# Conversion of the channel weights in 256-column pieces, spread over two token mixings, with two of its operations on ScalarE

## The chip, the cores and the metric

One core of a Trainium2 chip runs the whole program. The metric is device time in microseconds of one execution, the median of several. The engines named here: TensorE (PE) multiplies matrices into PSUM, VectorE (DVE), ScalarE (ACT) and GpSimd (POOL) work element by element, SyncE (SP) issues DMAs; ScalarE's queue issues some too. Every engine takes its own instructions in the order in which they are queued; semaphores hold an instruction until what it needs is there.

## What is computed

The reference has three stages, one behind the other, on 4 batches of 576 tokens and 512 columns: windowed attention, a mixture of four attention experts, and a mixing layer. The change lies in the last one:

```python
def _moe2_ref(x, w_theta, w_tok_r, w_tok_i, w_ch) -> np.ndarray:
    theta = x @ w_theta
    cos_t, sin_t = (np.cos(theta), np.sin(theta))
    zr = x * cos_t
    zi = x * sin_t
    yr = np.einsum('ts,bsd->btd', w_tok_r, zr)
    yi = np.einsum('ts,bsd->btd', w_tok_i, zi)
    y = yr + yi
    u = x + y
    return (u + np.maximum(u @ w_ch, 0.0)).astype(np.float32)
```

`w_ch`, the channel weights, is 512x512. Its inputs here are 64-bit floating-point numbers, and so are those of `w_theta` and of the token weights.

## The kernel before

Every product is made of three matmuls (`mm3`, L92 to L95): both operands are split into a high part and a low part (`split`, L85 to L90, or the end of `load64`), and high x high, high x low and low x high add up in PSUM. So each operand of a product costs a cast and a subtraction on the helper engines.

The mixing layer works per batch b and per half dh of the columns. `x_split(b)` makes high and low parts of x (tiles cx: L89 on VectorE, L90 on GpSimd). `theta(b, dh)` (L469 to L519) does blocks i of 128 tokens: the angle in PSUM (th, 12 matmuls), a transposed x (xk, a pair of transposes, L486), the fraction of the angle (ang, L490 and L492 on VectorE), sine and cosine on ScalarE (L493 to L495), their products with x (zf, L508 or L517 on VectorE), and the split of these into z (L87 on ScalarE, L90 on GpSimd). `mix(b, dh)` (L521 to L542) multiplies the z blocks by the token weights wkh, wkl into four PSUM banks (y, 108 matmuls), adds them to x on VectorE (L541) and splits the sum (tiles cu). `channel(b)` (L544 to L557) multiplies the sum by the channel weights wch, wcl, of which two of the four row blocks lie in the tiles wd.

`load64` (L100 to L132) turns 64-bit weights into a high and a low 32-bit part. A DMA brings a piece into the tile st (names w64c for the channel weights, w64k for token weights, w64t for theta weights); `lo` and `hi` are its 32-bit halves. Then:

- L115 on GpSimd or L117 on ScalarE: t = hi scaled (`KN["DM"][kind]` decides)
- L118 on ScalarE: u = lo scaled
- L119 and L120 on VectorE: t shifted, and the sign put back
- L122 on GpSimd: t += u, as integers
- L125 on VectorE or L127 on ScalarE: the high part, a cast of t (`KN["DH"][kind]`)
- L128: the low part, t minus the high part (`KN["DL"][kind]`, VectorE for the channel weights)

`KN["DP"][kind]` says into how many column parts a piece is cut for these. Kind 0 is theta, 1 token, 2 channel weights; the token weights go in rows of 576 columns. `load_ch` (L577 to L587) loads the channel weights in eight pieces k of 256 columns. Even and odd pieces have one buffer each: st and t, u of an even piece lie together in one tile (tag bmsx, named w64c), those of an odd piece in two tiles (tags VD0 and VD1, named w64c and wtuc). So a piece's load waits for the end of the piece two before it. The loads are issued from ScalarE's queue (L103).

What is put side by side is decided by `merge` (L45): it draws from generators in turn by their declared costs, which gives the program order and the order in which buffers are handed out. A scheduler of the framework then orders each engine's queue by its own estimate of when an instruction could start. Before the change, all eight pieces are merged with the first mixing:

```python
        todo = [(KN["TC"][4], mix(b, 0)), (KN["TC"][b % 2], theta(b, 1))]
        if b == 0:
            todo.append((KN["CW"][3], load_ch()))
        merge(*todo)
```

In names such as zf0121 or ang012 the digits are b, dh and the block i; in w64c6 and wtuc7 the digit is the piece.

Of the kernel before, what the change touches and what calls it, by code (L numbers as in the profile page):

```python
# [23 lines left out]
DM = H * D  # L24
E = 4
NP = H // 2
KN = {'AT': [12.51, 2.36, 85.51, 5.66, 48.01, 55.86, 30.7, 4.07], 'QK': [16.78, 11.97, 9.28, 7.37, 6.82, 0.65, 9.6, 19.46, 20.6], 'VG': [6.74, 4.28, 3.79, 19.87], 'WO': [16.49, 4.2, 5.44, 88.79], 'PA': [20.87, 6.19, 12.47, 3.34, 11.04, 2.93, 5.67], 'TW': [1.13, 0.05, 2.9, 0.49, 1.86], 'CW': [14.78, 12.49, 0.79, 3.08, 1.4, 0.05, 1.33], 'SC': [5, 4, 3, 3, 0, 5, 1, 1], 'BD': [2, 1, 2, 1], 'PV': [0, 1, 1, 1], 'VB': [4, 0, 0, 2], 'WB': [0, 0, 0, 1], 'SB': 2, 'TB': 3, 'WOI': 0, 'AS': [0, 2, 1, 2], 'WE': [[0, 0], [0, 3], [0, 1]], 'XE': [0, 1, 1, 0], 'QB': [0, 1, 0, 0, 0, 0, 0, 0], 'DM': [1, 0, 1], 'DH': [1, 0, 1], 'DL': [0, 0, 1], 'BC': [1, 0, 1, 1], 'LT': 2, 'DP': [1, 1, 2], 'KC': 0, 'WM': 448, 'TC': [6.98, 7.5, 7.5, 7.5, 20.8, 9.0]}
NZ = 7
CT = ("tb", "bs")
WARM = 2  # L30
# [10 lines left out]
def f32(ap):  # L41
    return ap.bitcast(F32)


def merge(*parts):  # L45

    live = [[0.0, float(total), gen] for total, gen in parts]
    while live:
        p = min(live, key=lambda x: x[0] / x[1])
        cost = next(p[2], None)  # L50
        if cost is None:
            live.remove(p)
        else:
            p[0] += cost
# [3 lines left out]
def kernel(ctx, tc, qT, kT, vw, consts, w_in, w_o, w_th, w_tk, w_ch, outT):  # L58
# [41 lines left out]
    def load64(kind, st, tu, dst_h, dst_l, src, scale=1.0):  # L100
# [7 lines left out]
        lo, hi = v[:, :, 0], v[:, :, 1]  # L108
        n = KN["DP"][kind]
        step = st.shape[1] // n  # L110
        full = lo, hi, tu[:, 0], tu[:, 1], dst_h, dst_l
        for k in range(n):
            lo, hi, t, u, dst_h, dst_l = (x[:, step * k : step * k + step] for x in full)
            if KN["DM"][kind]:
                nc.gpsimd.tensor_scalar(out=f32(t), in0=f32(hi), scalar1=2.0**-112, scalar2=1.0, op0=ALU.mult, op1=ALU.mult)  # L115
# [141 lines left out]
    QS, KA, VG, GW, O = {}, {}, {}, {}, {}  # L257
# [263 lines left out]
    def mix(b, dh):  # L521
        x2 = x2T[b]
        if dh == 0:
            UH[b] = hl_set(utags, f"cu{b}")
        uh, ul = UH[b]
        y = [bank([P, 288], tag, f"y{b}{dh}{k}") for k, tag in enumerate(("g", "g", "as", "ta"))]
        for c in range(9):
            zt = Z[b, dh, c // 2]
            q = c % 2 if c < 8 else 0
            for k in range(4):  # L530
                n, mm = divmod(k, 2)
                sl = slice(288 * n, 288 * n + 288)
                ms = slice(mm * P, mm * P + P)
                mm3(y[k], zt[:, q, 0, ms], zt[:, q, 1, ms], wkh[c][:, sl], wkl[c][:, sl],
                    c == 0, c == 8)
            yield 1.45
        for k in range(4):
            n, mm = divmod(k, 2)
            m = 2 * dh + mm
            sl = slice(288 * n, 288 * n + 288)  # L540
            nc.vector.tensor_add(out=x2[:, m, sl], in0=y[k], in1=x2[:, m, sl])  # L541
            split(uh[m][:, sl], ul[m][:, sl], x2[:, m, sl], nc.scalar, nc.gpsimd)  # L542
# [34 lines left out]
    def load_ch():  # L577
        for k in range(2 * NC):
            c, sl = k // 2, slice(HW * (k % 2), HW * (k % 2) + HW)
            if k % 2:  # L580
                st = bp.tile([P, HW], U64, tag="VD0", name=f"w64c{k}")
                tu = bp.tile([P, 2, HW], U32, tag="VD1", name=f"wtuc{k}")
            else:
                su = rp.tile([P, 2, HW], U64, tag="bmsx", name=f"w64c{k}")
                st, tu = su[:, 0], su[:, 1].bitcast(U32).rearrange("p (two n) -> p two n", two=2)
            load64(2, st, tu, wch[c][:, sl], wcl[c][:, sl], w_ch[c * P : (c + 1) * P, sl])
            yield 0.5  # L587
# [17 lines left out]
    for b in range(B):  # L605
        todo = [(KN["AT"][2 * b], attn(b, 0)), (KN["QK"][2 * b], qk(b, 1))]
# [25 lines left out]
        todo = [(KN["AT"][2 * b + 1], attn(b, 1))]  # L632
# [17 lines left out]
    wd = [bp.tile([P, 2, DM], F32R, tag="vg", bufs=2, name=f"wd{c}") for c in range(2)]  # L650
    wch = [wc[0], wc[2], wd[0][:, 0], wd[1][:, 0]]
    wcl = [wc[1], wc[3], wd[0][:, 1], wd[1][:, 1]]
    for b in range(B):
        todo = [(KN["TC"][4], mix(b, 0)), (KN["TC"][b % 2], theta(b, 1))]
        if b == 0:
            todo.append((KN["CW"][3], load_ch()))
        merge(*todo)
        if b < B - 1:
            x_split(b + 1)
            merge((KN["TC"][4], mix(b, 1)), (KN["TC"][2 + b % 2], theta(b + 1, 0)))  # L660
        else:
            merge((13, mix(b, 1)))
        merge((12, channel(b)))
# [55 lines left out]
```

## Time and profile before

| | before |
|---|---|
| median of 3 runs | 552.16 us (551.96 to 552.63) |
| profiled execution | 552.61 us, its span 550.7 us |
| PE busy | 519.8 us, 94% |
| DVE busy | 367.4 us, 67% |
| ACT busy | 319.1 us, 58% |
| POOL busy | 302.8 us, 55% |
| TensorE clock granted, mean | 0.981 of full speed |

The profiled execution is one run; its span goes from the first to the last instruction that the profile shows, and the rest of its time lies around that. The shares are means over stages with different limits, so the rows below are taken from the stretch in which the channel weights are converted, some 317 to 359 us after the span's start. An engine is shown as busy while an instruction runs or stands in a port; on TensorE shown lengths overlap, since the next matmul starts before the last has drained.

### The profile page before, as it was taken

To read this page: it belongs to the slowest core of one execution; us is meant where nothing else is said; L and a number is where in the kernel's file an instruction comes from. 1 tells how busy PE (TensorE), PEld (TensorE's weight loads), DVE (VectorE), ACT (ScalarE), POOL (GpSimd) and SP (SyncE) were. 2 spreads that over 40 slices of the span, in tenths; PEclk is the share of its full clock that TensorE was granted. 3 is DMA by queue.
4 is the path that set the end of the run, shared out by engine and by line. 5 is a ranking of instruction groups with operands and counts; after the bars stand their busy time and mean duration, and the time that the engine had idled before them with its cause. 6 is when DMAs were issued, how large, how long until landed. Compare 5 with 4: busy or idle time off the path is not lost.

```text
span 550.7 us, 12516 instructions
## 1 busy us (share of the span) xinstructions
PE 519.8 (94%) x4372; PEld 483.6 (88%) x4372; DVE 367.4 (67%) x1394; ACT 319.1 (58%) x1023; POOL 302.8 (55%) x479
## 2 busy tenths in 40 slices
PE   7799999999999999998898998699999999999997
PEld 5679878898987899988787997599999999999997
DVE  5796889858888688659999699953453535443312
ACT  6967687855778667777657955343343414442410
POOL 5786697635757653238565586943364514651420
PEclk9979999999999999999799899989999999999999
DMA  8754233323124331104004112001100110011002
GB/s 273 221 161 134 74 101 89 91 75 106 38 75 130 98 121 32 30 3 129 1 2 149 63 39 72 7 1 35 53 2 0 34 55 1 1 33 55 1 1 87
DMA packets 20799, 36.81 MB, mean 67 GB/s; under 512 B 2304, under 2 KB 13056, under 8 KB 20736
## 3 DMA queue, kind: packets, MB, share of 16 engines
q1 hardware_dynamic: 19008, 31.55, 18.5%
q10 hardware_dynamic: 1728, 4.46, 2.5%
q8 instruction: 35, 0.57, 0.5%
q14 instruction: 28, 0.23, 0.1%
HBM read 31.28 MB, written 4.72 MB: 65 GB/s over the span
## 4 chain that ended last, share of the span: by engine, by line
PE 69%; DVE 18%; ACT 4%; DMA 3%; POOL 3%; issue 3%; SPq 1%; POOLq 0%; ACTq 0%; DVEq 0%
PE y L94 6%; PE y L93 6%; PE y L95 6%; PE as L214 4%; PE ao L249 3%; PE c L94 3%; PE c L95 3%; PE c L93 3%; PE o L424 3%; PE th L93 3%; PE th L95 3%; PE th L94 3%; PE apt L239 2%; PE bpt L409 2%; PE qk L93 2%
## 5 line engine op out<-in xcount | busy, mean ns | idle before, releaser
L90 POOL TENSOR_TENSOR z<-zf,z 128x256 fp32r<-128x256 f32 x72 | 52.9, 751 | 89.8 <-ACT z L87 89.7
L93 PE MATMUL y<-wkh,z 128*128 128x288 f32 x288 | 86.9, 303 | 0.3 <-DVE x2T L541 0.3
L94 PE MATMUL y<-wkl,z 128*128 128x288 f32 x288 | 85.8, 298 | 0.0
L95 PE MATMUL y<-wkh,z 128*128 128x288 f32 x288 | 85.0, 299 | 0.0
L227 ACT ACTIVATE ams<-ams,anm 128x128 f32<-128x128 f32 x144 | 56.9, 398 | 7.6 <-DVE anm L219 6.3
L493 ACT ACTIVATE ang<-ang 128x256 f32<-128x256 f32 x36 | 14.6, 416 | 74.4 <-DVE ang L492 74.2
L93 PEld LDWEIGHTS y<-wkh,z 128*128 128x128 f32 x288 | 54.8, 190 | 0.8 <-DVE x2T L541 0.8
L94 PEld LDWEIGHTS y<-wkl,z 128*128 128x128 f32 x288 | 54.8, 190 | 0.0
L95 PEld LDWEIGHTS y<-wkh,z 128*128 128x128 f32 x288 | 54.4, 190 | 0.0
L384 ACT ACTIVATE bms<-bms,bnm 64x64 f32<-64x64 f32 (+4 forms) x80 | 44.7, 561 | 14.1 <-DVE bnm L376 7.0
L82 POOL TENSOR_SCALAR QD<-qt 64x192 f32<-64x192 f32 x72 | 39.2, 545 | 23.8 <-PE as L214 20.5
L234 POOL TENSOR_TENSOR ams<-ams,arc 128x384 f32<-128x384 f32 x48 | 40.2, 838 | 22.1 <-DVE arc L233 8.1
L87 ACT CAST z<-zf 128x256 fp32r<-128x256 f32 x72 | 27.2, 404 | 40.5 <-PE y L95 15.6
L214 PE MATMUL as<-kt,QD 128*128 128x128 f32 x288 | 43.6, 288 | 4.4 <-ACT QD L209 3.6
L214 PEld LDWEIGHTS as<-kt,QD 128*128 128x128 f32 x288 | 36.3, 192 | 8.8 <-ACT QD L209 3.9
L376 DVE CUSTOM_DVE_ANT_0 bms<-bs,mb 128x288 f32<-128x288 f32 (+4 forms) x96 | 38.8, 426 | 5.8 <-PE bs L374 3.3
L508 DVE TENSOR_TENSOR zf<-xk,ang 128x256 f32<-128x256 f32 x64 | 24.8, 417 | 25.1 <-ACT ang L495 21.1
L93 PE MATMUL th<-wth,cx 128*128 128x256 f32 x128 | 36.5, 286 | 3.8 <-DVE ang L492 3.7
L219 DVE CUSTOM_DVE_ANT_0 ams<-as,cst 128x128 f32<-128x128 f32 x144 | 34.5, 283 | 6.4 <-PE apt L239 5.0
L554 DVE SCALAR_TENSOR_TENSOR x2T<-c,x2T 128x288 f32<-128x288 f32 x32 | 14.4, 456 | 34.6 <-PE c L95 34.5
L94 PE MATMUL th<-wtl,cx 128*128 128x256 f32 x128 | 36.0, 282 | 0.0
L490 DVE TENSOR_SCALAR ang<-th 128x256 f32<-128x256 f32 x36 | 15.1, 420 | 31.2 <-PE th L95 30.9
(196 smaller groups left out, 1778.0 us busy)
## 6 DMA issues: line engine op xcount, KB each, us to landing
vt<-in_dram SPq DMA_DIRECT2D x48, 192.0 KB, 2.4
kt<-in_dram SPq DMA_DIRECT2D x16, 320.0 KB, 3.6
qt<-in_dram SPq DMA_DIRECT2D x16, 288.0 KB, 3.2
out_dram<-x2T SPq DMA_DIRECT2D x32, 144.0 KB, 1.8
w64k<-in_dram SPq DMA_DIRECT2D x5, 576.0 KB, 3.8
w64k<-in_dram ACTq DMA_DIRECT2D x4, 576.0 KB, 3.7
w64t<-in_dram SPq DMA_DIRECT2D x4, 512.0 KB, 4.8
w64c<-in_dram ACTq DMA_DIRECT2D x8, 256.0 KB, 2.8
```

Source lines behind the costliest of these rows:

```text
L82: nc.gpsimd.tensor_scalar(out=out, in0=in_, scalar1=by, scalar2=1.0, op0=ALU.mult, op1=ALU.mult)
L87: nc.scalar.copy(out=dst_h, in_=src)
L90: eng_l.tensor_sub(out=dst_l, in0=src, in1=f32(dst_h))
L93: nc.tensor.matmul(out, wh, xh, start=first, stop=False)
L94: nc.tensor.matmul(out, wh, xl, start=False, stop=False)
L95: nc.tensor.matmul(out, wl, xh, start=False, stop=last)
L214: nc.tensor.matmul(s[:, i, :], QD[g][:, i], kt[:, 64 * blk : 64 * blk + 128], start=True, stop=True)
L219: nc.vector.tensor_tensor_reduce(out=ms[:, i, :], in0=s[:, i, :], in1=ma0 if (g == 0 and i == 0) else ma1, scale=-0.125, scalar=3.0e38, op ...
L227: nc.scalar.activation(out=ms[:, i, :], in_=ms[:, i, :], func=AF.Exp, bias=nm[:, i : i + 1], scale=-1.0, accum_out=sm[:, i : i + 1],)
L234: nc.gpsimd.tensor_mul(out=ms, in0=ms, in1=rc.unsqueeze(2).to_broadcast([P, 3, P]))
L376: nc.vector.tensor_tensor_reduce(out=ms[:m, a:z], in0=s[:m, : z - a], in1=mb[:m, mo + a : mo + z], scale=-0.125, scalar=3.0e38, op0=ALU.ad ...
L384: ex = nc.scalar.activation(out=ms[:m, :w], in_=ms[:m, :w], func=AF.Exp, bias=nm[:m, 0:1], scale=-1.0, accum_out=sm[:m, i : i + 1])
```

## The change

Three entries of the table KN change, each for kind 2, the channel weights: `'DM'` from `[1, 0, 1]` to `[1, 0, 0]` (the scaling of hi goes from GpSimd, L115, to ScalarE, L117), `'DH'` from `[1, 0, 1]` to `[1, 0, 0]` (the cast goes from VectorE, L125, to ScalarE, L127), and `'DP'` from `[1, 1, 2]` to `[1, 1, 1]` (256 columns in one instruction, not twice 128). And `load_ch` is drawn from in two merges, three pieces in the first and the rest in the second:

```diff
@@ -650,14 +650,18 @@
     wd = [bp.tile([P, 2, DM], F32R, tag="vg", bufs=2, name=f"wd{c}") for c in range(2)]
     wch = [wc[0], wc[2], wd[0][:, 0], wd[1][:, 0]]
     wcl = [wc[1], wc[3], wd[0][:, 1], wd[1][:, 1]]
+    ch = load_ch()
     for b in range(B):
         todo = [(KN["TC"][4], mix(b, 0)), (KN["TC"][b % 2], theta(b, 1))]
         if b == 0:
-            todo.append((KN["CW"][3], load_ch()))
+            todo.append((KN["CW"][3], islice(ch, 3)))
         merge(*todo)
         if b < B - 1:
             x_split(b + 1)
-            merge((KN["TC"][4], mix(b, 1)), (KN["TC"][2 + b % 2], theta(b + 1, 0)))
+            todo = [(KN["TC"][4], mix(b, 1)), (KN["TC"][2 + b % 2], theta(b + 1, 0))]
+            if b == 0:
+                todo.append((KN["CW"][3], ch))
+            merge(*todo)
         else:
             merge((13, mix(b, 1)))
         merge((12, channel(b)))
```

On VectorE, the end of the first mixing and the split of the next batch's x, where the last pieces are converted. Before:

```order
L541 TENSOR_TENSOR x2T0_68<-y003_5297,x2T0_68 128x288
L120 SCALAR_TENSOR_TENSOR w64c6_5673<-w64c6_5673 128x128
L89 CAST cx10_5706<-x2T1_69 128x512
L125 CAST wd1_5285<-wtuc7_5690 128x128
L89 CAST cx12_5708<-x2T1_69 128x512
L128 TENSOR_TENSOR wd1_5285<-wtuc7_5690,wd1_5285 128x128
L89 CAST cx14_5710<-x2T1_69 128x512
L490 TENSOR_SCALAR ang012_5508<-th013_5576 128x256
L125 CAST wd1_5285<-w64c6_5673 128x128
L128 TENSOR_TENSOR wd1_5285<-wtuc7_5690,wd1_5285 128x128
L490 TENSOR_SCALAR ang014_5655<-th014_5639 128x256
L492 TENSOR_TENSOR ang012_5508<-th013_5576,ang012_5508 128x256
```

After, from the same addition on:

```order
L541 TENSOR_TENSOR x2T0_68<-y003_5297,x2T0_68 128x288
L89 CAST cx10_5602<-x2T1_69 128x512
L89 CAST cx12_5604<-x2T1_69 128x512
L89 CAST cx14_5606<-x2T1_69 128x512
L508 TENSOR_TENSOR zf0120_5494<-xk012_5484,ang012_5487 128x256
L508 TENSOR_TENSOR zf0121_5498<-xk012_5484,ang012_5487 128x256
L490 TENSOR_SCALAR ang012_5487<-th013_5538 128x256
L128 TENSOR_TENSOR wd1_5285<-w64c6_5827,wd1_5285 128x256
L490 TENSOR_SCALAR ang014_5584<-th014_5568 128x256
L492 TENSOR_TENSOR ang012_5487<-th013_5538,ang012_5487 128x256
L492 TENSOR_TENSOR ang014_5584<-th014_5568,ang014_5584 128x256
```

Of the conversion one subtraction is left behind the addition of y003, where five instructions of it stood in these rows and more behind them; the casts L125 are gone, and the two products zf012 now stand behind the casts of cx, where they stood just ahead of this addition.

On ScalarE, where the last two pieces are loaded and scaled. Before:

```order
L87 CAST z010_5332<-zf0100_5333 128x256
L87 CAST z010_5332<-zf0101_5337 128x256
L118 ACTIVATE wtuc7_5690<-w64c7_5689 128x128 x2
L103 DMA w64c6_5673<-in_8_dram 128x256
L87 CAST z011_5431<-zf0110_5432 128x256
L87 CAST z011_5431<-zf0111_5436 128x256
L493 ACTIVATE ang012_5508<-ang012_5508 128x256
L118 ACTIVATE w64c6_5673<-w64c6_5673 128x128 x2
L494 ACTIVATE ang012_5508<-ang012_5508 128x256
L495 ACTIVATE ang012_5508<-ang012_5508,halfpi_64 128x256
```

After, the same place:

```order
L127 CAST wd0_5284<-w64c4_5699 128x256
L117 ACTIVATE wtuc7_5903<-w64c7_5902 128x256
L118 ACTIVATE wtuc7_5903<-w64c7_5902 128x256
L495 ACTIVATE ang010_5326<-ang010_5326,halfpi_64 128x256
L87 CAST z010_5332<-zf0101_5337 128x256
L103 DMA w64c6_5827<-in_8_dram 128x256
L87 CAST z011_5417<-zf0110_5418 128x256
L87 CAST z011_5417<-zf0111_5422 128x256
L117 ACTIVATE w64c6_5827<-w64c6_5827 128x256
L118 ACTIVATE w64c6_5827<-w64c6_5827 128x256
L127 CAST wd1_5285<-wtuc7_5903 128x256
```

The load of piece 6 (L103) now stands behind both scalings of piece 7, and behind it come L117, L118 and the cast L127, in one queue with the casts of z and the sines.

On GpSimd, from the first split of the sum (cu) in batch 0 to the third z block. Before:

```order
L115 TENSOR_SCALAR w64c6_5673<-w64c6_5673 128x128 x2
L122 TENSOR_TENSOR wtuc7_5690<-wtuc7_5690 128x128 x2
L90 TENSOR_TENSOR cu01_5287<-x2T0_68,cu00_5286 128x288
L122 TENSOR_TENSOR w64c6_5673<-w64c6_5673 128x128
L90 TENSOR_TENSOR cu03_5289<-x2T0_68,cu02_5288 128x288
L90 TENSOR_TENSOR cu01_5287<-x2T0_68,cu00_5286 128x288
L90 TENSOR_TENSOR cx17_5713<-x2T1_69,cx16_5712 128x512
L90 TENSOR_TENSOR z012_5514<-zf0120_5515,z012_5514 128x256
L90 TENSOR_TENSOR z012_5514<-zf0121_5519,z012_5514 128x256
L122 TENSOR_TENSOR w64c6_5673<-w64c6_5673 128x128
L90 TENSOR_TENSOR cu03_5289<-x2T0_68,cu02_5288 128x288
L90 TENSOR_TENSOR cx11_5707<-x2T1_69,cx10_5706 128x512
```

After, from the add of piece 6 on:

```order
L122 TENSOR_TENSOR w64c6_5827<-w64c6_5827 128x256
L90 TENSOR_TENSOR cu01_5287<-x2T0_68,cu00_5286 128x288
L90 TENSOR_TENSOR cu03_5289<-x2T0_68,cu02_5288 128x288
L90 TENSOR_TENSOR cx17_5609<-x2T1_69,cx16_5608 128x512
L90 TENSOR_TENSOR cx11_5603<-x2T1_69,cx10_5602 128x512
L90 TENSOR_TENSOR cu01_5287<-x2T0_68,cu00_5286 128x288
L90 TENSOR_TENSOR cx13_5605<-x2T1_69,cx12_5604 128x512
L90 TENSOR_TENSOR cu03_5289<-x2T0_68,cu02_5288 128x288
L90 TENSOR_TENSOR cx15_5607<-x2T1_69,cx14_5606 128x512
L90 TENSOR_TENSOR z012_5493<-zf0120_5494,z012_5493 128x256
L90 TENSOR_TENSOR z012_5493<-zf0121_5498,z012_5493 128x256
```

The add of piece 6 is one instruction and stands ahead of all splits, where two halves of it were spread among them; the third z block now stands behind the splits of cx.

## Rows read from the trace of the kernel before

**Rows 1.** Page, part 2: busy tenths of TensorE and VectorE, granted clock, in 40 slices

```profile
PE   7799999999999999998898998699999999999997
...
DVE  5796889858888688659999699953453535443312
...
PEclk9979999999999999999799899989999999999999
```

**Rows 2.** Two stretches: from:to, length, busy PE, PEld, DVE, ACT, POOL (instructions), clock, DMA

```profile
321.40:358.00 36.60, 29.30 (x216) 27.58 (x215) 36.26 (x92) 16.75 (x50) 30.05 (x51) 0.99 0.14 44
375.00:550.70 175.70, 172.56 (x1339) 172.32 (x1337) 67.49 (x160) 55.80 (x141) 65.74 (x82) 1.00 0.08 28
```

**Rows 3.** TensorE's timeline: start, length, line, output <- inputs, shape [idle before]

```profile
321.53 0.38 PE L93 MATMUL y<-wkh,z 128*128 128x288 f32 x1
...
332.76 0.30 PE L93 MATMUL y<-wkh,z 128*128 128x288 f32 x1
...
335.68 0.29 PE L94 MATMUL y<-wkl,z 128*128 128x288 f32 x1
...
352.22 0.29 PE L95 MATMUL y<-wkh,z 128*128 128x288 f32 x1
356.23 0.38 PE L93 MATMUL th<-wth,cx 128*128 128x256 f32 x1 [3.72 <-DVE ang L492]
...
358.43 0.44 PE L93 MATMUL y<-wkh,z 128*128 128x288 f32 x1
358.67 0.44 PE L94 MATMUL y<-wkl,z 128*128 128x288 f32 x1
...
361.06 0.38 PE L486 MATMUL xk<-cst,x2T 128*128 128x128 f32 x2
```

**Rows 4.** One stretch, busy by line, in turn L119, L120, L125, L128, L115, L122, L118

```profile
317.10:358.60 41.50, 7.13 (x16) 0.98 0.13 39
...
317.10:358.60 41.50, 5.89 (x16) 0.98 0.13 39
...
317.10:358.60 41.50, 7.42 (x16) 0.98 0.13 39
...
317.10:358.60 41.50, 8.76 (x16) 1.41 (x1) 0.98 0.13 39
...
317.10:358.60 41.50, 4.77 (x16) 0.98 0.13 39
...
317.10:358.60 41.50, 7.57 (x16) 0.98 0.13 39
...
317.10:358.60 41.50, 4.05 (x16) 0.98 0.13 39
```

**Rows 5.** Groups of the page's part 5, then by tile (min/median/max ns)

```profile
L90 POOL TENSOR_TENSOR z<-zf,z 128x256 fp32r<-128x256 f32 x72 | 52.9, 751 | 89.8 <-ACT z L87 89.7
...
L87 ACT CAST z<-zf 128x256 fp32r<-128x256 f32 x72 | 27.2, 404 | 40.5 <-PE y L95 15.6
...
L508 DVE TENSOR_TENSOR zf<-xk,ang 128x256 f32<-128x256 f32 x64 | 24.8, 417 | 25.1 <-ACT ang L495 21.1
...
L119 DVE TENSOR_SCALAR w64c<-w64c x8: 210/314/1420, 317.3 to 346.2; 128x128 uint32<-128x128 uint32 x8
...
L120 DVE SCALAR_TENSOR_TENSOR w64c<-w64c x8: 276/280/565, 318.9 to 348.8; 128x128 uint32<-128x128 uint32 x8
...
L119 DVE TENSOR_SCALAR wtuk<-wtuk x9: 445/450/1090, 246.8 to 311.4; 128x576 uint32<-128x576 uint32 x9
```

**Rows 6.** ScalarE's timeline, two loads of pieces; page, part 6, the loads

```profile
322.98 0.33 ACTq L103 DMA_DIRECT2D w64c<-in_dram  x1
...
342.45 0.33 ACTq L103 DMA_DIRECT2D w64c<-in_dram  x1
...
w64c<-in_dram ACTq DMA_DIRECT2D x8, 256.0 KB, 2.8
```

**Rows 7.** VectorE's timeline, one cast of the split of x

```profile
349.00 1.02 DVE L89 CAST cx<-x2T 128x512 fp32r<-128x512 f32 x1
```

More of the change, by code (lines that the diff above doesn't have):

```diff
@@ L26 @@
 NP = H // 2
-KN = {'AT': [12.51, 2.36, 85.51, 5.66, 48.01, 55.86, 30.7, 4.07], 'QK': [16.78, 11.97, 9.28, 7.37, 6.82, 0.65, 9.6, 19.46, 20.6], 'VG': [6.74, 4.28, 3.79, 19.87], 'WO': [16.49, 4.2, 5.44, 88.79], 'PA': [20.87, 6.19, 12.47, 3.34, 11.04, 2.93, 5.67], 'TW': [1.13, 0.05, 2.9, 0.49, 1.86], 'CW': [14.78, 12.49, 0.79, 3.08, 1.4, 0.05, 1.33], 'SC': [5, 4, 3, 3, 0, 5, 1, 1], 'BD': [2, 1, 2, 1], 'PV': [0, 1, 1, 1], 'VB': [4, 0, 0, 2], 'WB': [0, 0, 0, 1], 'SB': 2, 'TB': 3, 'WOI': 0, 'AS': [0, 2, 1, 2], 'WE': [[0, 0], [0, 3], [0, 1]], 'XE': [0, 1, 1, 0], 'QB': [0, 1, 0, 0, 0, 0, 0, 0], 'DM': [1, 0, 1], 'DH': [1, 0, 1], 'DL': [0, 0, 1], 'BC': [1, 0, 1, 1], 'LT': 2, 'DP': [1, 1, 2], 'KC': 0, 'WM': 448, 'TC': [6.98, 7.5, 7.5, 7.5, 20.8, 9.0]}
+KN = {'AT': [12.51, 2.36, 85.51, 5.66, 48.01, 55.86, 30.7, 4.07], 'QK': [16.78, 11.97, 9.28, 7.37, 6.82, 0.65, 9.6, 19.46, 20.6], 'VG': [6.74, 4.28, 3.79, 19.87], 'WO': [16.49, 4.2, 5.44, 88.79], 'PA': [20.87, 6.19, 12.47, 3.34, 11.04, 2.93, 5.67], 'TW': [1.13, 0.05, 2.9, 0.49, 1.86], 'CW': [14.78, 12.49, 0.79, 3.08, 1.4, 0.05, 1.33], 'SC': [5, 4, 3, 3, 0, 5, 1, 1], 'BD': [2, 1, 2, 1], 'PV': [0, 1, 1, 1], 'VB': [4, 0, 0, 2], 'WB': [0, 0, 0, 1], 'SB': 2, 'TB': 3, 'WOI': 0, 'AS': [0, 2, 1, 2], 'WE': [[0, 0], [0, 3], [0, 1]], 'XE': [0, 1, 1, 0], 'QB': [0, 1, 0, 0, 0, 0, 0, 0], 'DM': [1, 0, 0], 'DH': [1, 0, 0], 'DL': [0, 0, 1], 'BC': [1, 0, 1, 1], 'LT': 2, 'DP': [1, 1, 1], 'KC': 0, 'WM': 448, 'TC': [6.98, 7.5, 7.5, 7.5, 20.8, 9.0]}
 NZ = 7
```

## The prediction

> **What bounds the kernel now.** I read the page's forty slices first, then the busy time of two stretches, then TensorE's timeline with its waits. In slices 24 to 26 (about 317 to 358 us) VectorE shows 9 and TensorE falls from 9 to 6; after that TensorE stays at 9 into the last slice and VectorE at 5 or below [rows 1]. The stretches say the same: from 321.4 to 358.0 VectorE is busy 36.26 of 36.6 us and TensorE 29.30; from 375 on TensorE is busy 172.56 of 175.7 [rows 2]. So VectorE bounds one stretch of some 37 us, and TensorE everything behind it: a microsecond won back in the stretch is a microsecond off the end, one won later is none.
>
> How much is to be won? TensorE's longest wait there, 3.72 us, is for the angle of L492 [rows 3]. Busy time hides part of the loss, since a matmul's shown length overlaps the next, so I count from start to start. An undisturbed y matmul of 288 columns comes every 0.133 us (332.76 to 335.68 is 22 steps), a theta matmul of 256 columns by width every 0.118. From the first y matmul at 321.53 to the transpose pair at 361.06, 39.5 us, TensorE did 159 y matmuls (21.1), 52 theta matmuls (6.1) and seven transpose pairs (1 to 1.5): 28.5 us of work, 11 us lost [rows 3]. The loss has two kinds: waits for VectorE (4.0 us from 352.22 to 356.23 alone), and, behind that long wait, a stretch at the lower clock, 1.2 instead of 2.4 GHz, in which a y matmul takes 0.24 instead of 0.133 us (358.43 to 358.67), some 1.5 us over fourteen of them [rows 1, 3].
>
> **The change part by part.** *VectorE.* Before, eight pieces in two halves give 16 instructions each of L119, L120, L125 and L128: 7.13 + 5.89 + 7.42 + 8.76 = 29.2 us of the stretch's 41.5 [rows 4]. After, the cast L125 is ScalarE's, and 8 each of L119, L120 and L128 remain, twice as wide: 64 instructions become 24. Undisturbed, L119 costs 0.21 us at 128 columns and 0.445 at 576, so 0.28 at 256; L120 costs 0.276 at 128 and, like the 256-column zf of L508, 0.41 to 0.42 at 256; L128 reads two SBUF sources like L120, so the same [rows 5]. That is 8 x (0.28 + 0.42 + 0.42) = 9.0 us as the lower bound. The sixteen sets of before would undisturbed be 16 x (0.21 + 0.276 + 0.21 + 0.276) = 15.6, so 13.6 us of the 29.2 were stretching, 0.21 per instruction. If the stretching goes with the count: 9.0 + 24 x 0.21 = 14 us. If it goes with the length: 9.0 x 29.2/15.6 = 16.8, the upper bound. I take 14, because the same L119 at 576 columns has a median hardly over its minimum (450 against 445) while at 128 it has 314 against 210 and up to 1420: it is not length that stretches [rows 5]. VectorE is thus relieved of about 15 us (12 to 20) in the stretch that it bounds.
>
> A 128-column L119, 210 ns at best, took up to 1420 [rows 5]. The Trainium skill (SBUF — State Buffer, Who interferes with whom) calls the port pair that VectorE shares with GpSimd an exclusive lock, held for a whole instruction while the other blocks. That speaks against wider pieces: all three instructions left can meet the lock, and the GpSimd add that blocks them grows from 0.47 to 0.75 us. By that rule the 0.21 would grow to 0.34 and the 14 us to 17, at the upper bound, and the gain by some 2 us smaller, inside the range; the 1420 ns agree that whole instructions block.
>
> *GpSimd* loses the 16 multiplies of L115 (4.77 us) and does 8 adds of 256 columns for 16 of 128: by the 0.751 us of its 256-column z instruction 6.0 for 7.57 [rows 4, 5]. It gets 6.3 us back.
>
> *ScalarE* does 8 multiplies L117, 8 L118 and 8 casts L127 of 256 columns at the 0.404 us of its z cast: 9.7 us for the 4.05 of before [rows 4, 5]. The 5.7 us more lie beside 16.75 busy of 36.6 us [rows 2], so they cost nothing as a sum. As an order they do: L117 now waits at the head of ScalarE's queue for a piece's load, with z casts and sines queued behind it.
>
> *The spread.* Three pieces belong to the first mixing and five to the second now. The order shows that this moves little: the scheduler sets pieces 3 to 7 where they stood, the last one still in front of the angles of the fourth and fifth theta blocks on VectorE. I cost it at nothing either way (at most one piece, 3 x 0.6 = 1.8 us of VectorE). No DMA is added; the eight loads stay on ScalarE's queue, 2.8 us from issue to landing each [rows 6].
>
> **What is late next.** Two pieces are under way at a time, each in its own buffer, so a load waits until the piece two before is done. Even pieces were loaded at 322.98 and, two trips later, at 342.45: 9.7 us a trip [rows 6]. A trip of after is at least 2.8 (landing) + 0.40 (L117) + 0.28 + 0.42 (L119, L120) + 0.75 (add) + 0.40 (cast) + 0.42 (L128) = 5.5 us; on VectorE a pair of zf (0.83) and of angle steps (0.83) queue between, and z work on ScalarE and GpSimd, so I take 7.8. From 322.98, itself 1.5 earlier since the first piece loses a pair of VectorE steps, the last load is issued at 321.5 + 2 x 7.8 = 337.1 to 338.5 with some queueing behind L117 on ScalarE; I take 338.5, or 8.5 us a trip.
>
> Now VectorE in the new order: landing 341.3, L117 to 341.7, then L119, four additions L541 (0.47 by width), L120 and a stretched L128 to 344.9. Three casts L89, 1.02 us in the row, say 0.9, make 347.6, two zf 348.4; L490, L128, L490, L492 make 350.4 [rows 5, 7]. TensorE gets to the second half's first y matmul at 321.5 + 108 x 0.133 + 48 x 0.118 + six transpose pairs = 342.6. It waits there for the banks that L541 frees (0.9 us in all), stands before the transpose of the fifth block at 346.3 until 348.5 (2.1), and before the first theta block of batch 1 from 349.8 to 350.4 (0.6). So 3.6 us of waits remain, with small ones 4, none long enough to be like the 4.0 us behind which the clock fell. Lost before 11, after 4: **7 us won**. Behind the stretch TensorE is full as before, and the helpers have as much room as before, so all of it arrives at the end. The weights are then ready at about 350, with most of the second mixing's 108 matmuls (14 us) still to come before the channel stage asks for them.
>
> **The rivals.** *The last load comes no earlier* (342.3, two trips of 10.4, where before has 9.7): because L117 makes ScalarE wait for each load, and the next load is issued from that same queue. Everything that hangs on it is 3.8 us later, gain 3.2: 549. For it: loads are issued in order with z casts. Against it: each trip loses two VectorE steps and half its instructions.
>
> *TensorE becomes the bound sooner.* If casts and conversions are hardly stretched, the waits shrink. GpSimd then limits: behind the last add (343.1) stand four cu (0.84 each by width), four cx (1.5) and the first z of the third block (0.75), to 353, where TensorE by the reckoning above arrives at 355. So at most 2 us more: gain 9, 543.2.
>
> *ScalarE's queue turns the change into a loss.* If a trip grows past 12 us (the 7 us spread over two trips on the 8.5 of the forecast), because z casts stand behind L117 and L117 behind a load, the waits in front of the theta block cost more than now; at 13 us a trip it ends 2 us slower, 554.2. For it: 24 conversion instructions on one in-order queue where there were 16 short ones. Against it: ScalarE sits half idle there and its waits are for VectorE.
>
> *The change doesn't do what it says*: the pieces stay in place by the order, and if VectorE's relief were swallowed by stretching, the time would stay at 552.2. Against it: 40 instructions are gone from a full engine.
>
> **How the numbers follow.** The profiled execution took 552.61 us (span 550.7), the median of the runs is 552.16. 552.61 - 7.0 = 545.6, and set against the median 545.2, which I give. Chances: forecast 0.60 (gain 5.5 to 8.5), last load no earlier 0.15, TensorE sooner the bound 0.15, no effect 0.05, slower 0.05. The range from 542.5 to 549.5 takes in the first three with their bounds, VectorE's 12 to 20 us among them, and leaves out little over 0.1. What can be told from no change is about 0.2%, 1.1 us: faster 0.90, the same 0.05, slower 0.05.
>
> **What the changed profile would show.** Right: L119, L120 and L128 of the pieces together 14 us on VectorE (9 to 17) in 24 instructions; the last load at 338.5; TensorE's wait for L492 under 1 us; the clock full around 350; the first channel matmul some 7 us earlier than before. Wrong: the last load at 342 or later (the first rival); z casts that wait on ScalarE behind L117 while TensorE waits for z (the third); or later waits on TensorE behind 358, which would give back what the stretch won.

## The result and the profile after

The changed kernel takes 547.26 us (median; 546.12 to 548.62), the kernel before 552.14 beside it: ratio 0.9905 (0.9877 to 0.9932). The gain is 4.9 us by the medians, 5.9 by the profiled executions (546.72 against 552.61). The forecast was 7.0 us: the sign and the range hold, and the gain is smaller.

The page of the changed kernel, part 2, answers to [rows 1]: slices 24 to 26, where VectorE stood at 9 and TensorE fell to 6, are at 8, 6, 8 and 9, 9, 7, and behind them TensorE is at 9 as before.

```profile
PE   7879999999999999999799899799999999999997
...
DVE  5886898857888688658989868863354435443412
...
PEclk8989999999999999999799899999999999999999
```

The two stretches of [rows 2], with the same columns (the second starts at the same time and ends with the span):

```profile
321.40:358.00 36.60, 33.08 (x257) 32.25 (x256) 29.36 (x61) 21.50 (x61) 29.84 (x36) 1.00 0.14 45
375.00:544.70 169.70, 166.50 (x1293) 166.26 (x1291) 65.47 (x156) 54.48 (x138) 64.21 (x80) 1.00 0.08 28
```

VectorE has come down from 36.26 to 29.36 us, ScalarE has gone up from 16.75 to 21.50, and TensorE does 257 recorded matmuls in the stretch where it did 216. The conversion's part of VectorE, by line L119, L120 and L128 (busy time and count), answers to [rows 4]; L125 has no row any more:

```profile
317.10:375.00 57.90, 3.21 (x8) 1.00 0.09 31
...
317.10:375.00 57.90, 4.93 (x8) 1.00 0.09 31
...
317.10:375.00 57.90, 5.60 (x8) 1.27 (x1) 1.00 0.09 31
```

That is 13.7 us for 29.2. ScalarE's three lines of it (L117, L118, L127) take 3.52 + 3.40 + 3.17 = 10.1 us, GpSimd's add L122 5.92. The last load, from ScalarE's queue, and TensorE's waits from 310 to 400 us (sum, times, longest):

```profile
338.62 0.33 ACTq L103 DMA_DIRECT2D w64c<-in_dram  x1
...
PE xk L486 <- DVE zf L508: 2.7, 1, 2.7
PE th L93 <- DVE ang L492: 0.5, 1, 0.5
PE y L93 <- DVE x2T L541: 0.3, 1, 0.3
```

Where before the longest wait was the 3.72 us for L492 [rows 3], now it is one of 2.7 us for a product zf, in front of the transposes of the fifth theta block. VectorE's timeline says why, with GpSimd's beside it:

```profile
344.07 0.81 DVE L541 TENSOR_TENSOR x2T<-y,x2T 128x288 f32<-128x288 f32 x2
344.80 3.90 DVE L89 CAST cx<-x2T 128x512 fp32r<-128x512 f32 x3
348.62 0.74 DVE L508 TENSOR_TENSOR zf<-xk,ang 128x256 f32<-128x256 f32 x2
349.28 0.41 DVE L490 TENSOR_SCALAR ang<-th 128x256 f32<-128x256 f32 x1
349.61 1.27 DVE L128 TENSOR_TENSOR wd<-w64c,wd 128x256 fp32r<-128x256 f32 x1
...
351.14 0.74 DVE L492 TENSOR_TENSOR ang<-th,ang 128x256 f32<-128x256 f32 x2
...
345.52 2.89 POOL L90 TENSOR_TENSOR cx<-x2T,cx 128x512 fp32r<-128x512 f32 x2
```

The two zf (zf012) stand behind the three casts of cx, and these take 3.90 us while GpSimd subtracts. In the kernel before, the two zf come ahead of these casts, the first of which is the row of [rows 7] at 349.00:

```profile
347.76 0.74 DVE L508 TENSOR_TENSOR zf<-xk,ang 128x256 f32<-128x256 f32 x2
```

How the gain is told apart from what varies between executions: the stretch is measured in every run below from TensorE's first y matmul to its first channel matmul (c). Before, these are at 321.53 and 374.56, 53.0 us apart; after:

```profile
321.73 0.38 PE L93 MATMUL y<-wkh,z 128*128 128x288 f32 x1
...
368.50 0.38 PE L93 MATMUL c<-cu,wch 128*128 128x288 f32 x1
```

46.8 us apart. From the first c to the end of the run's time it is 178.05 us before and 178.22 after. It lies between 177.9 and 178.4 in all the runs below too, so nothing that is won ahead of the channel stage is given back behind it. The first y itself lies anywhere from 320.1 to 321.9 (320.36 in a kernel whose queues are those of before), so a microsecond between two single executions says nothing; the distance y to c is what to compare. It varies too, and most kernels have one profile only: 53.0 and 53.5 us where the queues are those of before, 46.8, 47.7 and 48.2 where they are those of the changed kernel.

### The profile page after: what moved, and what is told of

Its sections match the earlier page's. It is cut to its first block, busy times and chain, and to the rows that moved or that the text cites. A ratio compares the mean times of both kernels' runs of the same rounds, so it can differ in the third digit from the quotient of the medians.

```text
span 544.7 us, 12460 instructions
## 1 busy us (share of the span) xinstructions
PE 518.1 (95%) x4372; PEld 483.2 (89%) x4372; DVE 357.3 (66%) x1354; ACT 323.7 (59%) x1031; POOL 298.7 (55%) x455
## 4 chain that ended last, share of the span: by engine, by line
PE 69%; DVE 15%; ACT 4%; POOL 4%; DMA 4%; issue 3%; SPq 1%; ACTq 0%; POOLq 0%; DVEq 0%
PE y L94 6%; PE y L93 6%; PE y L95 6%; PE as L214 4%; PE c L94 3%; PE c L95 3%; PE c L93 3%; PE ao L249 3%; PE o L424 3%; PE th L93 3%; PE th L95 3%; PE th L94 3%; PE apt L239 2%; PE bpt L409 2%; PE qk L93 2%
## 5 line engine op out<-in xcount | busy, mean ns | idle before, releaser
L93 PEld LDWEIGHTS y<-wkh,z 128*128 128x128 f32 x288 | 54.1, 188 | 0.6 <-DVE x2T L541 0.6
L95 PEld LDWEIGHTS y<-wkh,z 128*128 128x128 f32 x288 | 53.9, 188 | 0.0
L214 PE MATMUL as<-kt,QD 128*128 128x128 f32 x288 | 45.5, 298 | 3.6 <-ACT QD L209 2.7
L214 PEld LDWEIGHTS as<-kt,QD 128*128 128x128 f32 x288 | 38.4, 203 | 7.8 <-ACT QD L209 3.1
L508 DVE TENSOR_TENSOR zf<-xk,ang 128x256 f32<-128x256 f32 x64 | 25.1, 419 | 28.1 <-ACT ang L495 17.9
L90 POOL TENSOR_TENSOR cu<-x2T,cu 128x288 fp32r<-128x288 f32 x32 | 26.1, 836 | 17.8 <-ACT cu L87 17.8
```

Of the source, the lines that this page charges most:

```text
L90: eng_l.tensor_sub(out=dst_l, in0=src, in1=f32(dst_h))
L93: nc.tensor.matmul(out, wh, xh, start=first, stop=False)
L95: nc.tensor.matmul(out, wl, xh, start=False, stop=last)
L214: nc.tensor.matmul(s[:, i, :], QD[g][:, i], kt[:, 64 * blk : 64 * blk + 128], start=True, stop=True)
```

## The experiments

Entries of the table KN are shown alone; what differs in each list is its last number, that of kind 2. The edits are against the changed kernel where nothing else is said.

**Is it the spread?** The change without it: all eight pieces are merged with the first mixing, the table as changed.

```diff
-            todo.append((KN["CW"][3], islice(ch, 3)))
+            todo.append((KN["CW"][3], ch))
...
-            if b == 0:
-                todo.append((KN["CW"][3], ch))
```

> The three table entries of the change, but all eight pieces merged with the first mixing as before. Theory (the spread moves nothing, the gain is VectorE's relief): the same queue orders as the changed kernel, so its time, 546 to 548.6 us, 5 us under before, VectorE 13.7 us on L119, L120 and L128, the last load near 338.6. Rival (the spread carries part of the gain): at least 1.1 us slower than the changed kernel, a ratio to before above 0.993.

Measured: 546.13 us, ratio 0.9898 (0.9881 to 0.9915), the last load at 338.7, a wait of 2.7 us for zf. Every engine's queue holds the same instructions in the same order as with the spread, but for one load that changes places with a copy beside it on ScalarE, at 321 us. And the spread alone, on the table of before:

> Only the spread, three and five pieces, with the table entries of before. Theory: nothing moves, 552.1 us, ratio 1.000 within 0.001, VectorE again 29 us on the conversion. Rival (spreading the load thins out VectorE's stretch): 549 to 551 us.

Measured: 552.83 us, ratio 0.9996 (0.998 to 1.0012); here the queues are those of before, but for one load that stands three places earlier on ScalarE, at 313 us. So the spread does nothing that can be measured, and the whole effect is the table's three entries.

**Does the gain go with VectorE's relief?** The change with pieces in two halves again:

```diff
-'DP': [1, 1, 1],
+'DP': [1, 1, 2],
```

> The change with pieces cut in two halves of 128 columns again, cast and scaling still on ScalarE: 48 instructions on VectorE, 8 each of L119, L120 and L128 doubled. Theory (the stretching goes with the count): 16 x (0.21 + 0.276 + 0.276) + 48 x 0.21 = 22 us on VectorE, half of the relief, so about 549.5 us, between the two kernels. Rival (it is the move of the cast to ScalarE that pays, the width costs nothing): within 1 us of the changed kernel, about 547.

Measured: 546.34 us, ratio 0.9895 (0.9878 to 0.9912). VectorE's conversion is 4.98 + 7.98 + 7.85 = 20.8 us in 48 instructions, near the 22 expected by the count. But the time is the rival's, that of the changed kernel, although 7 us of the relief are gone. Either the last part of the relief is worth nothing, or the changed kernel pays for it elsewhere; the runs below ask which.

**Is it the casts of cx?** The changed kernel with the casts of the split of x for batch 1 on ScalarE:

```diff
-            split(XH[b][0][c][:, :W4], XH[b][1][c][:, :W4], x2T[b][:, c, :W4], nc.vector, nc.gpsimd)
+            split(XH[b][0][c][:, :W4], XH[b][1][c][:, :W4], x2T[b][:, c, :W4], nc.scalar if b == 1 else nc.vector, nc.gpsimd)
```

> The changed kernel with the four casts of the split of x for batch 1 (L89) on ScalarE instead of VectorE. In the changed kernel three of them take 3.9 us on VectorE ahead of the products zf012, and TensorE waits 2.69 us for these before the transpose of the fifth block. Theory (that stretching is what is left of the stretch's loss): that wait falls below 1 us, 1.5 to 2.5 us faster than the changed kernel, about 545. Rival (GpSimd's subtractions for cu and cx and z012, to 354.2 us, are the bound behind it): the wait moves to the third z block and the time stays at 547.

Measured: 541.48 us (540.72 to 542.23), ratio 0.9806 (0.9788 to 0.9823): by the ratio 10.7 us less than before, and 4.7 less than the 546.13 beside it. It is the fastest kernel of this study, and the gain is well over what either expectation allowed. TensorE's one wait from 310 to 400 us (it lies ahead of the first y), its stretch (columns as in [rows 2]), the lines on VectorE that the waits hung on, and the moved casts on ScalarE (min/median/max ns):

```profile
PE xk L486 <- DVE zf L508: 0.2, 1, 0.2
...
316.60:358.60 42.00, 41.69 (x330) 40.90 (x327) 29.16 (x71) 28.89 (x84) 32.43 (x40) 1.00 0.12 39
...
341.14 0.81 DVE L541 TENSOR_TENSOR x2T<-y,x2T 128x288 f32<-128x288 f32 x2
341.98 0.76 DVE L508 TENSOR_TENSOR zf<-xk,ang 128x256 f32<-128x256 f32 x2
...
343.89 0.42 DVE L492 TENSOR_TENSOR ang<-th,ang 128x256 f32<-128x256 f32 x1
...
L87 ACT CAST cx<-x2T x4: 615/616/663, 318.4 to 343.5; 128x512 fp32r<-128x512 f32 x4
```

The zf come straight behind the last L541, the last L492 at 343.89 where the changed kernel has the pair at 351.14, and TensorE is busy 41.69 of 42 us. From the first y to the first c TensorE waits nowhere and its clock is full: these 42.6 us are what the work there takes by itself. Now the same casts of cx on ScalarE, on the kernel before:

> The kernel before, conversion untouched, with only the four casts of the split of x for batch 1 on ScalarE. VectorE loses 0.4 + 1.0 + 1.0 + 0.7 = 3.1 us in its full stretch. Theory P: 1 us under before, ratio 0.998. Theory H: the handoff is not the bound while the conversion keeps VectorE full to 358 us, so at most the 3.1 us taken away, ratio 0.995. Rival (the split casts are what holds TensorE in both kernels): as large a step as on the changed kernel, 4.7 us, ratio 0.9915.

Measured: 550.20 us, ratio 0.9953 (0.9937 to 0.997), as theory H had it. Alone it is worth 2.6 us, on top of the change nearly 5: with the conversion still at 27.0 us of VectorE, TensorE goes on waiting there (2.3 us for L492, 2.1 in four places in front of transposes).

**Each entry taken back, and each alone.** Without the cast's move:

```diff
-'DH': [1, 0, 0],
+'DH': [1, 0, 1],
```

> The change with the cast of the high part back on VectorE (32 instructions of 256 columns there, the scaling still on ScalarE). VectorE by the count: 9.0 + 8 x 0.28 + 32 x 0.21 = 18 us, a relief of 11. Theory P (the gain goes in proportion to VectorE's relief, 5.5 us for 15.5): 4 us under before, ratio 0.993. Theory H (from a relief of some 8 us on, the handoff between the two mixings is the bound: the additions, the split casts of x stretched by GpSimd, the angles): as the changed kernel, ratio 0.990.

Measured: 545.45 us, ratio 0.987 (0.9852 to 0.9887); VectorE's conversion 18.0 us as expected, and the time below both theories (0.993 and 0.990). The cast alone, on the kernel before (`'DH': [1, 0, 0]`):

> The kernel before with one thing changed, the cast of the high part on ScalarE (halves of 128 columns, scaling on GpSimd): 48 instructions on VectorE as in the run with two halves, 21 us by that run, a relief of 8, and GpSimd keeps its 4.8 us of scalings. Theory P: 3 us under before, ratio 0.995. Theory H: as the changed kernel, ratio 0.990; if GpSimd's scalings matter, between the two.

Measured: 551.30 us, ratio 0.9981 (0.9968 to 0.9994): less gain than either theory gave (0.995 and 0.990). The conversion is 23.5 us for the 21 expected. The scaling alone, on the kernel before (`'DM': [1, 0, 0]`):

> The kernel before with one thing changed, the scaling on ScalarE instead of GpSimd: VectorE keeps its 64 instructions, GpSimd loses 4.8 us. Both theories with stretching by the count: VectorE stays at about 29 us and full, time 0 to 1 us under before, ratio 0.998 to 1.000. Rival: fewer GpSimd instructions stretch VectorE less, 25 us or below there, and the time falls by 2 us or more, ratio 0.996 or below.

Measured: 550.99 us, ratio 0.9973 (0.9958 to 0.9988), nearer to the theories' 0.998 than to the rival's 0.996; the conversion, 27.2 us, lies between their 29 and its 25. Here, too, zf012 stands behind the casts of cx, and TensorE waits long for it:

```profile
PE xk L486 <- DVE zf L508: 4.8, 3, 2.9
...
350.36 1.52 DVE L89 CAST cx<-x2T 128x512 fp32r<-128x512 f32 x1
351.79 0.74 DVE L508 TENSOR_TENSOR zf<-xk,ang 128x256 f32<-128x256 f32 x2
```

Two entries that give about a microsecond each and six together (the run with two halves) looked like two engines that both had to be relieved. That was put to the test with the scaling back on GpSimd, cast and width as changed:

```diff
-'DM': [1, 0, 0],
+'DM': [1, 0, 1],
```

> The changed kernel with only the scaling of hi back on GpSimd (L115, 256 columns); cast on ScalarE, whole-width pieces and the spread stay. Theory G (the stretch before was short of two engines, VectorE 40.9 and GpSimd 34.7 of 42 us busy; relief of one of them alone is worth about 1 us, as the cast alone and the scaling alone showed, and the two together 6): GpSimd gets back about 4.5 us less of its 6.3, so although VectorE is relieved by 15 us the gain is only 1 to 3 us: 549.5 to 551.5. Rival V (what counts is how much of VectorE's conversion is taken away; the two single edits were too small, 2 and 6 us): VectorE's conversion at 14 us as in the changed kernel, gain as there, 545.5 to 547. Rows: GpSimd's busy time in 316.6 to 358.6 (above 34 by G), the last load, TensorE's waits.

Measured: 544.91 us, ratio 0.987 (0.9846 to 0.9893). The theory of two engines (G) fell: GpSimd is busier than before, 35.23 of 42 us against 34.67, and the time is no longer than that of the changed kernel, by the medians of one chip (544.91 against 546.50 for the changed kernel once more, below) rather shorter, though their intervals overlap. VectorE's conversion is 4.52 + 4.68 + 5.02 = 14.2 us, half a microsecond above that of the changed kernel; the order behind it differs (last, what GpSimd does beside the casts):

```profile
343.79 0.75 DVE L508 TENSOR_TENSOR zf<-xk,ang 128x256 f32<-128x256 f32 x2
344.45 0.45 DVE L541 TENSOR_TENSOR x2T<-y,x2T 128x288 f32<-128x288 f32 x1
344.81 2.82 DVE L89 CAST cx<-x2T 128x512 fp32r<-128x512 f32 x3
...
348.55 0.74 DVE L492 TENSOR_TENSOR ang<-th,ang 128x256 f32<-128x256 f32 x2
...
PE xk L486 <- DVE zf L508: 1.7, 2, 0.9
PE th L93 <- DVE ang L492: 1.1, 1, 1.1
...
344.99 0.92 POOL L122 TENSOR_TENSOR w64c<-w64c 128x256 int32<-128x256 int32 x1
345.87 1.48 POOL L90 TENSOR_TENSOR cx<-x2T,cx 128x512 fp32r<-128x512 f32 x1
```

zf012 stands ahead of the casts of cx, and there is no wait in front of the fifth block's transposes (both waits for zf are earlier); the casts take 2.82 us for 3.90, beside one add and one subtraction where the changed kernel has two subtractions. The width alone, on the kernel before (`'DP': [1, 1, 1]`):

> The kernel before with only the width changed: eight pieces of 256 columns in one instruction each, scaling on GpSimd, cast on VectorE, all eight pieces in the first mixing. VectorE then has 32 instructions for 64. By the count (0.28 + 0.42 + 0.28 + 0.42 at best, plus 0.21 each) 11.2 + 6.7 = 17.9 us, relief 11; GpSimd's L115 and L122 fall from 12.3 to some 9.5. Theory G (both engines must be relieved): both are, in part, so 2 to 4 us of gain, 548.5 to 550.5. Rival V (VectorE's relief decides, in steps: 6 us gives 1, 8 gives 6, 11 gives 7): 545 to 546.5. If the gain is under 1 us, neither holds and the width counts only beside the scaling's move.

Measured: 548.54 us, ratio 0.993 (0.9909 to 0.9952). VectorE's conversion is 4.62 + 4.71 + 4.96 + 6.31 = 20.6 us, not 17.9: an instruction is stretched by 0.29 us here, not 0.21. The time is at the edge of what G gave, though the scaling back on GpSimd has ruled G out, and well above V's 545 to 546.5: the relief, 8.6 us for the 11 reckoned, is worth 3.9 us by the ratio. The cast back on VectorE and cx on ScalarE together:

> The changed kernel with the cast of the pieces back on VectorE (L125, 256 columns) and the casts of cx of batch 1 (L89) on ScalarE. VectorE's conversion about 17.7 us as when the cast alone was put back; the cx casts' 3.9 us gone from VectorE. If the handoff in front of zf012 and L492 is all that is left (theory C), TensorE's waits are gone here too and the time is as in the run with cx on ScalarE alone, 541 to 542.5. Rival: with ScalarE at 25 instead of 29 of 42 us busy the casts of cx and of z come sooner there, 539.5 to 541; or VectorE at 33 us puts zf012 behind the fourth instruction of the last piece and a wait of 1 to 2 us stays, 543 to 544.

Measured: 546.56 us, ratio 0.9899 (0.9877 to 0.9922): slower than each of the expectations, and than the kernel with the cast back alone (0.9870). The move of the casts of cx that gained 4.7 us on the changed kernel and 2.6 on the kernel before gains nothing here:

```profile
PE th L93 <- DVE ang L492: 1.7, 1, 1.7
...
345.50 0.74 DVE L508 TENSOR_TENSOR zf<-xk,ang 128x256 f32<-128x256 f32 x2
346.16 1.11 DVE L125 CAST wd<-w64c 128x256 fp32r<-128x256 f32 x1
347.20 1.52 DVE L128 TENSOR_TENSOR wd<-wtuc,wd 128x256 fp32r<-128x256 f32 x1
...
350.36 0.42 DVE L492 TENSOR_TENSOR ang<-th,ang 128x256 f32<-128x256 f32 x1
```

The place that the casts of cx had left is taken by L125 and L128 of the last two pieces, stretched by the same GpSimd subtractions, and L492, 30.0 us behind the first y, is as late as in the changed kernel (29.4). The conversion takes 21.7 us here, for 18.0 with the casts of cx on VectorE.

**The changed kernel once more.**

> The changed kernel once more, beside the others and the same runs of the kernel before. Its first result is 547.26 of four runs, and the run without the spread, whose queues are the same, gave 546.13: theory: it is one kernel, 546 to 547, a gain of 5.5 to 6.5 us. If it is 547.3 again, the spread costs a microsecond through something that the queues do not show. It also shows by how much the stretch starts earlier or later from execution to execution (the first y matmul at 321.7 so far, 320.1 to 321.5 in others).

Measured: 546.50 us (544.86 to 548.29), ratio 0.9892 (0.9865 to 0.9919). Its profiled execution is the longest of them, 548.29, y to c 48.2 us where the first profile had 46.8. TensorE's wait and the granted clock behind it, first this execution (columns of the last line as in [rows 2]):

```profile
350.10 0.41 PE L486 MATMUL xk<-cst,xt 128*128 128x128 f32 x2 [2.69 <-DVE zf L508]
...
352.00:354.00 2.00, 2.00 (x10) 1.79 (x9) 0.49 (x2) 1.81 (x6) 2.00 (x3) 0.50 0.00 0
```

and the first profile of the same kernel:

```profile
349.50 0.41 PE L486 MATMUL xk<-cst,xt 128*128 128x128 f32 x2 [2.69 <-DVE zf L508]
...
352.00:354.00 2.00, 2.00 (x18) 2.00 (x18) 0.42 (x1) 1.75 (x6) 2.00 (x3) 1.00 0.00 0
```

The wait is 2.69 us both times. Behind it the clock is granted at 0.50 in 352 to 354, the lower level of 1.2 GHz, in the one and is full in the other: 10 matmuls are recorded where 18 are. From these transposes to the first c it is 19.94 us (370.04 - 350.10) in the one, 19.00 in the other and 18.99 in the run without the spread, whose queues are the same: the fall costs 0.95 us. That is net: the wait of 0.5 us for L492 behind it is gone in this execution, since TensorE comes there later. The transposes themselves are 0.6 us later here and in the run without the spread (350.13). The last load and what waits for it tell why, first this execution, then the first profile:

```profile
338.70 0.33 ACTq L103 DMA_DIRECT2D w64c<-in_dram  x1
342.02 0.44 ACT L117 ACTIVATE w64c<-w64c 128x256 f32<-128x256 f32 x1 [0.73 <-DMA w64c<-in_dram]
...
342.49 0.30 DVE L119 TENSOR_SCALAR w64c<-w64c 128x256 uint32<-128x256 uint32 x1 [1.31 <-ACT w64c L117]
342.70 0.46 DVE L541 TENSOR_TENSOR x2T<-y,x2T 128x288 f32<-128x288 f32 x1
```

```profile
341.40 0.45 ACT L117 ACTIVATE w64c<-w64c 128x256 f32<-128x256 f32 x1 [0.21 <-DMA w64c<-in_dram]
...
341.88 0.31 DVE L119 TENSOR_SCALAR w64c<-w64c 128x256 uint32<-128x256 uint32 x1 [0.80 <-ACT w64c L117]
342.11 0.45 DVE L541 TENSOR_TENSOR x2T<-y,x2T 128x288 f32<-128x288 f32 x1
```

The load is issued 0.08 us later and lands 0.6 us later, ScalarE's L117 waits for it, VectorE stands at L119 for L117, and the additions L541 behind it are 0.6 us late, with the casts and zf012 after them. So the last landing is on the path, and in the first profile too: there VectorE stands 0.80 us at the same place. Why the load takes longer, no run shows.

**All together.** V, S and G are VectorE, ScalarE and GpSimd; the conversion is VectorE's busy time in all its instructions, y to c the distance defined above, the clock its granted mean from y to c, all three of the profiled execution; the ratio is the one given with each run.

| kernel | scaling | cast | columns | cast of cx | conversion | y to c | clock | ratio |
|---|---|---|---|---|---|---|---|---|
| before | G | V | 128 | V | 29.2 | 53.0 | 0.97 | 1 |
| scaling alone | S | V | 128 | V | 27.2 | 51.6 | 0.97 | 0.9973 |
| cast alone | G | S | 128 | V | 23.5 | 50.8 | 0.97 | 0.9981 |
| width alone | G | V | 256 | V | 20.6 | 49.8 | 0.97 | 0.9930 |
| two halves | S | S | 128 | V | 20.8 | 47.3 | 1.00 | 0.9895 |
| cast back | S | V | 256 | V | 18.0 | 46.9 | 1.00 | 0.9870 |
| scaling back | G | S | 256 | V | 14.2 | 45.3 | 1.00 | 0.9870 |
| spread alone | G | V | 128 | V | 29.8 | 53.5 | 0.97 | 0.9996 |
| changed, two profiles | S | S | 256 | V | 13.7, 13.6 | 46.8, 48.2 | 1.00, 0.96 | 0.9905, 0.9892 |
| without the spread | S | S | 256 | V | 13.7 | 47.7 | 1.00 | 0.9898 |
| cx alone | G | V | 128 | S | 27.0 | 50.4 | 0.97 | 0.9953 |
| cast back, cx | S | V | 256 | S | 21.7 | 47.9 | 1.00 | 0.9899 |
| changed, cx | S | S | 256 | S | 12.5 | 42.6 | 1.00 | 0.9806 |

The first seven rows go down together with the conversion but for one near tie: 15.0 us less of it make 7.8 us less from y to c, one half of a microsecond for each (0.37 to 0.70, each row against before). Part of that is TensorE's clock, which falls once between y and c in the first four profiles and not in the other three; a mean of 0.97 over some 50 us is about 1.6 us of full clock, and in the one pair of executions that shows it by itself the fall cost 0.95. Most of the 2.5 us by which width alone and two halves stand apart can be this. With it taken off, the 7.8 us become 6.2 to 6.8 (an estimate from these two figures), 0.41 to 0.46 us for each of relief.

The queues of the changed kernel are the exception. Their three profiles lie 1.5, 2.4 and, with the fall of the clock, 2.9 us above the scaling back, whose conversion is half a microsecond longer.

## Why the prediction came out as it did

**VectorE bounds the stretch, and about half of its relief arrives: right.** The reckoning of 15 us of relief for 7 us of gain is the slope of the table, with the clock's part in it, as the forecast had it. The kernel with the scaling left on GpSimd has the forecast's conversion (14.2 us for 14) and more than the forecast's gain from y to c (7.8 us), at 544.91 us. The changed kernel itself gained 4.9 us by the medians of the first result, less than the 5.5 to 8.5 that the prediction held likeliest; its profiled executions (5.9) and the repeat (6.0 by the ratio) lie inside.

**The terms.** VectorE's conversion was put at 14 us and is 13.7, so stretching by the count held here: (13.7 - 9.0)/24 = 0.20 us an instruction for 0.21. It isn't a constant: 0.29 with the width alone. The Trainium skill's rule (SBUF — State Buffer, Who interferes with whom), an exclusive lock for a whole instruction, would have made it 17 by the longer adds; the 13.7 speak against that use of it, though not against the lock (below). ScalarE's 10.1 us were put at 9.7, GpSimd's adds, 5.92, at 6.0. The last load was put at 338.5 and its landing at 341.3; it comes at 338.62 and L117 behind it starts at 341.40, so the first rival (no earlier than 342) is out, and with it the third, the jam in ScalarE's queue. The spread was costed at nothing, and is nothing.

**The waits: the right places, one term too small.** Foreseen were 2.1 us at the fifth block's transposes, 0.6 at the first theta block, 0.9 for banks; measured are 2.7, 0.5 and 0.3. The term that was mis-sized is the three casts of cx: 0.9 us each from the 1.02 of [rows 7], 1.3 each in the trace (3.90 for three). They start at 344.80 for a reckoned 344.9 and end 1.1 us late, and everything behind them is late by that: the transposes at 349.50 for 348.5, the theta block at 351.60 for 350.4. From the transposes to the first c it is 19.0 us, as the forecast of a c some 7 us earlier has it, so this is the 1.0 us between the 7.0 forecast and the 6.0 by which the span fell, 550.7 to 544.7. In before the casts stood apart, with the conversion between them, and GpSimd's subtractions were spread; in the changed kernel casts and subtractions of cx meet back to back, and the price was taken from a row of the looser order. The scaling back points to the neighbour and not to the closeness of the casts: its three casts are as close and cost 0.94 us each.

The waits themselves add up to 3.5 us for the 3.6 foreseen, and that is partly luck: TensorE too came later than reckoned, to the transposes at 346.8 for 346.3 and to the theta block at 351.1 for 349.8, and a later arrival shortens a wait. The loss can be measured against the 42.6 us of the kernel without waits: 10.4 us before and 4.2 after, where the prediction had 11 and 4. So its count of what is left came out, and its count of what was lost before was 0.6 us too high; by this count the rest of the 1.0 us is the 0.2 above 4 and a first y that comes 0.2 us later than reckoned.

**The clock: right in one execution, wrong in another.** The prediction had it stay full, since no wait was left like the 4.0 us behind which it fell. Behind the 2.69 us it fell in one execution and not in the other: with the fall the kernel took 548.29 us, without it 546.72, of which the fall is 0.95 and the later landing of the last load 0.6. Neither was foreseen as something that varies. How often each comes in the runs without a profile is not known; that they are a part of what spreads the changed kernel's times (544.86 to 548.29) is likely and not shown.

**What the prediction took for needed and is not.** It booked the whole gain on three entries that all help. Any two of them give as much as all three, or more (0.9895, 0.9870, 0.9870 against 0.9892 to 0.9905). Most of GpSimd's 6.3 us back is not needed, as the scaling back on GpSimd shows: there GpSimd keeps the scaling, 3.8 us, and gets back 2.7 us in all. The third entry brings its relief, and the queue order takes it away again: zf012 falls behind the casts of cx, while it stands ahead of them in the kernel before and in the kernels with the cast or the scaling back. The prediction saw this in the order and let it stand as a cost of 2.1 us; it did not say that it was the price of one particular combination. Shown are the order, the wait and the two kernels without it; no run changed the order of these five instructions and nothing else, so its price, 1.5 to 2.9 us, is the difference of two kernels that also differ in where the scaling is done. The scaling alone has the same order and a wait as long (2.9 us) without standing out in the table, since its wait for L492 is 0.4 us where before has 3.7; so what this order costs depends on what else the queue holds up.

**What was left to win** was in front of the transposes, the theta block and the banks, as the prediction said; with the casts of cx on ScalarE these 3.5 us of waits are gone in the trace, and y to c shrinks by 4.2. The second rival, GpSimd as the next bound at 353, was wrong: there GpSimd starts the third z block at 350.89, TensorE waits nowhere for it and y to c gains more than the 2 us allowed.

## What to carry to other kernels

Where a helper engine bounds a stretch, price its queue by instruction and by place: an operation beside a busy neighbour must be costed from rows in which the same neighbours run, and the order that an edit brings about can eat the gain of the edit. Try the parts of such a change singly and in pairs before keeping all of them, and compare the distance between two fixed points of the trace rather than whole times. When relief has been won, look at what stands in front of the last wait: here four casts moved to an engine with room were worth 4.7 us after the change, nearly as much as the change itself, 2.6 us before it, and nothing with the cast back on VectorE.

## What was not expected of the hardware

A cast of 512 columns takes 0.41 us on VectorE at its shortest and 1.53 at its longest in the changed kernel; GpSimd's subtraction of the same size takes 1.28 to 1.49 (min/median/max ns, whole run):

```profile
L89 DVE CAST cx<-x2T x16: 409/854/1528, 276.6 to 459.3; 128x512 fp32r<-128x512 f32 x16
L90 POOL TENSOR_TENSOR cx<-x2T,cx x16: 1282/1314/1485, 282.6 to 465.4; 128x512 fp32r<-128x512 f32 x16
```

So it is VectorE that pays when the two meet, and GpSimd little. In the changed kernel the three casts end at 345.85, 347.29 and 348.69, each 0.28 to 0.29 us behind the end of a GpSimd instruction (345.56, 347.01, 348.41), and take 1.05, 1.53 and 1.48 us; the two subtractions beside them take 1.49 and 1.44 us, the two behind them 1.30. The Trainium skill (SBUF — State Buffer, Who interferes with whom) has a cast on VectorE able to take the shared pair of ports and says that the pair is held for the whole instruction; these ends agree with that. It also says that ScalarE never waits on anyone: the same casts there take 0.615 to 0.663 us, slower than VectorE's best and half of what VectorE needs beside GpSimd.

TensorE's clock fell behind a wait of 2.69 us in one execution and not in another of the same kernel. Among the other profiles it fell, to a granted 0.50, behind waits of 3.72 us (before [rows 3]), 2.93 (scaling alone), 2.31 (cx alone), 2.18 (cast alone) and 1.83 (width alone), and stayed full behind 2.53 (two halves), 1.76 (cast back) and 1.74 (cast back with cx), and in the profile of the cast alone behind one of 3.06 us, further on (columns of the last line as in [rows 2]):

```profile
355.23 0.38 PE L93 MATMUL th<-wth,cx 128*128 128x256 f32 x1 [3.06 <-DVE ang L492]
...
355.00:360.00 5.00, 4.77 (x37) 4.77 (x38) 2.80 (x7) 2.88 (x8) 5.00 (x8) 1.00 0.00 0
```

So from 1.8 to 3.1 us the length of a wait did not tell here whether the clock would fall, and such a wait is best priced both with the fall and without, in this kernel 0.95 us apart.
